# Strided sparse attention and a Mish MLP: the order of batch 1's attention beside the first block's second multiplication

## The chip, the cores and the metric

The kernel runs on one core of a Trainium2 chip. The metric is the device time of one execution in microseconds (us); three runs of the kernel before are given by their median.

A core has a matrix engine (PE, with weight loads shown apart as PEld), a vector engine (DVE), a scalar engine (ACT), a general engine (POOL) and an engine that issues transfers (SP). Each carries out its own instructions in the order of the program, and waits on semaphores for the others.

## The reference

The sizes: 8 batches, 8 heads, 576 positions, head size 64. Heads 0 to 3 are local (a window of 32), heads 4 to 7 strided (every 32nd position).

```python
def _attn_ref(q, k, v):
    scores = scale * np.matmul(q, k.transpose(0, 1, 3, 2))
    rel = pos[:, None] - pos[None, :]
    mask_local = (rel >= 0) & (rel < stride)
    mask_strided = (rel >= 0) & (pos[None, :] % stride == pos[:, None] % stride)
    ...
    attn = np.exp(scores - np.max(scores, axis=-1, keepdims=True))
    attn = attn / (np.sum(attn, axis=-1, keepdims=True) + 1e-09)
    return np.matmul(attn, v)

def _moe_ref(x, w_in, w_out):          # x: 4608 tokens x 512
    h = x @ w_in                       # 512 x 2048
    sp = np.where(h > 20.0, h, np.log1p(np.exp(np.minimum(h, 20.0))))
    g = h * np.tanh(sp)                # Mish
    return g @ w_out                   # 2048 x 512
```

The output of the attention, heads side by side, is the x of the second function.

## The kernel before

The MLP runs over nine blocks of 512 tokens (`t` from 0 to 8). A batch has 576 tokens, so block 1 takes the last 64 tokens of batch 0 and the first 448 of batch 1, which are covered by five local tiles of 96. The attention of batch t + 1 is worked off between the matmul groups of block t. Block 0 multiplies plainly; later blocks use seven products instead of eight for each 2 x 2 split, with sums of weights (`sums_w`, into the tile Tw) and of inputs (`sums_x`, into Sx) prepared on VectorE.

There is no scheduler: the order of the source is the order on every engine. `mlp2` gives 16 groups of four matmuls for block 0 (line 781), and after group i the kernel issues the list `at[i]` that `attn_steps(1, y, y)` returns, with some steps appended:

```python
at[3] += [
    lambda: load_early_v_str(2), lambda: load_tiles_loc(2, kl, k),
    lambda: cast_v_loc(1, Po), lambda: load_tiles_loc(2, ql, q),
]
at[12].append(lambda: transpose_by_dma(2))
at[1].append(lambda: sums_w()[0](lo))
at[7].append(lambda: sums_w()[0](hi))
at[9].append(lambda: sums_w()[1](lo))
at[11].append(lambda: sums_w()[1](hi))
at[14].append(lambda: sums_x(1, "1"))
at[15] += [lambda: spread_v_str(2, Dv)]
```

The steps of batch 1's attention, with their lines:

- `t_step` transposes q or k on PE into a PSUM tile `tr` (strided, line 253: eight transposes; local, line 267: twelve), and one engine copies the tile into kTs, qTs, kTl or qTl (lines 197 and 199). Strided heads come as 72 x 72 pieces, local ones as 96 x 96. k and q of a pair of local heads (`hp` 0 or 1) are one step.
- `Q`, that is `qk`, makes a part of the scores on PE (line 333), in an accumulator of two PSUM banks or, with "t", in two single tiles, and ACT takes the exponential into P_s or P_l (line 347 for an accumulator, line 343, once for each tile, for "t"). The strided scores have three parts (432, 432 and 288 columns for each of two halves), the local ones three as well.
- `M`, that is `mask`, multiplies with the mask on VectorE (line 353).
- `V`, that is `pv`, multiplies with v on PE (line 369, tile `po`), then VectorE takes the reciprocal of the sums (line 380) and the product into x_s or x_l (line 381).
- `spread_v_str` copies v of the strided heads from vsr into vs (line 199); the next load of vsr waits for it.
- `X`, that is `xt`, transposes x_s or x_l on PE (lines 418 and 408, tile `trx`), and a copy puts it into xT, which the MLP reads. `xt_now(n)` does it for n of the six local tiles at once (line 433), and `xt_later(n)` has the rest done by transfers that transpose.

PSUM is scarce: `tile_t` gives one of two single banks in turn, `acc(i, ...)` a tile of two banks, of which there is one for each i. In block 0 both accumulators that `attn_steps` gets are the same one (x == y), and the branch `if x == y` serves this case alone. The kernel library follows reads and writes by tiles and sets the semaphore waits from them.

Of the kernel before, what the change touches and what calls it, by code (L numbers as in the profile page):

```python
# [11 lines left out]
BF16 = mybir.dt.bfloat16  # L12
# [5 lines left out]
WQ = 96  # L18
# [25 lines left out]
def kernel(ctx, tc, q, k, v, moe_w_in, moe_w_out, out):  # L44
    nc = tc.nc
# [13 lines left out]
    xT = const.tile([128, 4, RT], BF16, name="xT")  # L59
# [47 lines left out]
    def acc(i, name):  # L107

        pool = ps_z[0] if i == 2 else ps_a
        return pool.tile([128, 2, 512], F32, tag=f"acc{i}", name=name)  # L110
# [10 lines left out]
    def tile_t(name):  # L121
        return ps_t.tile([128, 512], F32, tag="pt", name=name)
# [11 lines left out]
    def by_head(x):  # L134

        return x[0:PL].rearrange("p j h d -> p (j h d)").rearrange("p (h x) -> p h x", h=4)
# [12 lines left out]
    def vs_raw():  # L149

        return vsr[0:PN]
# [4 lines left out]
    def spread_v_str(b, eng):  # L156
        cast(eng, vs[b % 2][0:PN, :, :, 0:D], vs_raw().rearrange("p h (j d) -> p h j d", d=D))
# [37 lines left out]
    def cast(eng, out_, in_):  # L195
        if eng is nc.scalar:
            nc.scalar.copy(out_, in_)  # L197
        else:
            eng.tensor_copy(out_, in_)
# [42 lines left out]
            eng.memset(vl[b % 2][0:32, 0, :, 0:D], 0.0)  # L242


    def t_step(b, kind, which, hp, eng=None):

        eng = eng or nc.vector
        tr = tile_t("tr")[:].bitcast(BF16)
        if kind == "s":
            src = (qs if which == "q" else ks)[b % 2]  # L250
            for u in range(8):
                h, jj = 2 * hp + u // 4, u % 4
                nc.tensor.transpose(  # L253
                    tr[:, PN * u:PN * u + PN],
                    src[0:PN, h, 128 * jj:128 * jj + 128],
                    ident[0:PN, 0:PN],
                )
            dst = (qTs if which == "q" else kTs)[:, 8 * SU * hp:8 * SU * hp + 8 * SU]
            cast(
                eng, dst.rearrange("c (u n) -> c u n", u=8)[:, :, 0:PN],  # L260
                tr[:, 0:S].rearrange("c (u n) -> c u n", u=8),
            )
        else:
            src = by_head((ql if which == "q" else kl)[b % 2])
            for j in range(CL):
                for e in range(2):
                    nc.tensor.transpose(  # L267
                        tr[64 * e:64 * e + 64, PL * j:PL * j + PL],
                        src[:, 2 * hp + e, D * j:D * j + D], ident[0:PL, 0:PL],
                    )  # L270
            dst = qTl[:, hp, :] if which == "q" else kTl[:, hp, 32:32 + S]
            cast(
                eng, dst.rearrange("c (p j) -> c p j", j=CL),
                tr[:, 0:S].rearrange("c (j p) -> c p j", j=CL),
            )
# [7 lines left out]
    T_ORDER = [(kd, w, hp) for kd in ("s", "l") for hp in range(2) for w in ("k", "q")]  # L283
# [10 lines left out]
    class Attn:  # L294
# [129 lines left out]
                    tr[:, 0:576].rearrange("p (j n) -> p n j", j=CS),  # L424
                )

        def xt_now(self, n):
            tr = tile_t("trx")[:].bitcast(BF16)
            t0 = (self.b % RING) * S
            for c in range(2):  # L430
                for w in range(n):
                    o = (n * c + w) * WQ
                    nc.tensor.transpose(
                        tr[:, o:o + WQ], x_l[0:WQ, w, 128 * c:128 * c + 128], ident[0:WQ, 0:WQ]
                    )
            cast(
                nc.scalar, xT[:, 0:2, t0:t0 + n * WQ],
                tr[:, 0:2 * n * WQ].rearrange("p (c n) -> p c n", c=2),
            )

# [6 lines left out]
    def attn_steps(b, x, y):  # L447

        a = Attn(b)
        Q = lambda i_acc, *parts: (lambda: a.qk(parts, i_acc))  # L450
        M = lambda kd, i: (lambda: a.mask(kd, i, nc.vector))
        V = lambda kd, i: (lambda: a.pv(kd, i))
        X = lambda kd, hf: (lambda: a.xt(kd, hf))
        s0, s1, sl2, l0, l1 = ("s", 0), ("s", 1), (("s", 2), ("l", 2)), ("l", 0), ("l", 1)
        if x == y:
            T = [(lambda n=n, eng=eng: t_step(b, *T_ORDER[n], eng)) for n, eng in enumerate(
                (None, None, None, None, None, nc.scalar, None, nc.scalar))]
            return [
                T[2:4], [Q(x, s0)],
                [M(*s0), Q(x, s1)],  # L460
                [lambda: spread_v_str(b, nc.vector), V("s", 0)],
                [V("s", 1), M(*s1), Q(x, ("s", 2))],
                [V("s", 2), T[4]],
                [V("s", 3), M("s", 2), T[5]],
                [V("s", 4), T[6]],
                [V("s", 5), T[7]],
                [V("s", 6), Q(x, l0)],
                [V("s", 7), M(*l0), Q(x, l1)],
                [X("s", 0), V("l", 0), M(*l1), Q(x, ("l", 2))],
                [X("s", 1), V("l", 1), M("l", 2)],  # L470
                [V("l", 2), V("l", 3)],
                [V("l", 4), V("l", 5)],
                [lambda hf=hf: a.xt("l", hf, nc.vector) for hf in range(2)],
            ], T[0:2]
        V2 = lambda kd, i, z: (lambda: a.pv2(kd, i, z))
        G = lambda kd, i: (lambda: a.mask(kd, i, nc.gpsimd))
        l2 = ("l", 2)
        now = -(-(512 * (b + 1) - S * b) // WQ)
        at = [
            [],  # L480
            [Q(x, s0), Q(y, s1), Q("t", *sl2), M(*s0), M(*s1), M("s", 2)],
            [],
            [V2("s", 0, y), G(*l2)],
            [],
            [V2("s", 2, y), Q(x, l0), Q("t", l1), G(*l0), G(*l1)],
            [],
            [V2("s", 4, y), lambda: nc.scalar.preload_act_table(AF.Mish)],
            [],
            [V2("s", 6, y)],
            [V2("l", 0, x)],  # L490
            [X("s", 0), V2("l", 2, y), X("s", 1)],
            [V2("l", 4, x), lambda: a.xt_now(now)],
            [lambda: a.xt_later(now)],
        ]
        return at
# [364 lines left out]
    with tc.manual_schedule():  # L860
# [43 lines left out]
        a = Attn(0)  # L904
        unread(16)
        cast(Dv, ks[0][0:PN, 0:2, :], st0)
        t_step(0, "s", "k", 0, Sc)
        unread(3, 2)
        t_step(0, "s", "k", 1, Sc)
        ps = [a.bias("s", i, i) for i in range(2)]  # L910
        unread(5, 2)
# [15 lines left out]
        ps = [a.bias("l", 0, 2)]  # L927
# [33 lines left out]
        for t in range(NBLK):  # L961
            if t == 0:
                x, y, z = accs
                at, ts = attn_steps(1, y, y)
                at[3] += [
                    lambda: load_early_v_str(2), lambda: load_tiles_loc(2, kl, k),
# [12 lines left out]
            else:  # L979
                if t == 1:  # L980
                    split_third()
                x, y = 0, 1
                gT, z, g1 = mlp1(t, (y, x) if t == 1 else (x, y))
                at = attn_steps(t + 1, x, y) if t + 1 < B else []
                if t == 1:
                    at[0].append(lambda: sums_w()[3](hi))
# [63 lines left out]
```

## Time and profile before

| what | us |
|---|---|
| median of three runs | 287.01 (286.88 to 287.05) |
| profiled execution | 286.68 |
| its span | 284.8 |
| block 0's second multiplication with batch 1's attention | 35.19 to 57.39 |
| granted clock of TensorE | 1.00 |

The profile is one execution. Its timeline lists instructions with start, duration, engine, line and operands, and in brackets the idle time before and what ended it; the chain of work that ended last is followed back from the last instruction. The shares of the span by engine tell which engine the chain lies on, and a wait counts only there. Starts of matmuls overlap by a little, since they are pipelined; steps are best measured from start to start.

The starts of the 16 groups of block 0 in us: 35.19, 36.58, 37.84, 39.25, 40.31, 41.63, 43.25, 44.72, 46.25, 47.71, 49.12, 50.63, 52.18, 53.45, 54.64, 56.01; block 1 begins at 57.39.

### The profile page before, as it was taken

Reading aid. Unit: us, or ns where it says so; the run is one execution under the profiler, and the core shown is the slowest. Engines: PE = TensorE matmul, PEld = TensorE weight load, DVE = VectorE, ACT = ScalarE, POOL = GpSimd, SP = SyncE. Lnnn points to the kernel's source line nnn. Section 1 sums busy time; section 2 is a strip of 40 time slices with the busy share of each in tenths; the row PEclk is TensorE's granted clock in tenths of the full one; section 3 lists DMA queues with packets and bytes.
Section 4 is the critical chain, followed back from the end, with each engine's and each line's share of the span. In section 5 each row is a group of like instructions: output and inputs, shape, how many; then the busy total and the mean of one; then the engine's idle time right before and its main releaser. Section 6 shows DMA issues by size and latency. Waiting matters only on the chain.

```text
span 284.8 us, 7535 instructions
## 1 busy us (share of the span) xinstructions
PE 279.0 (98%) x3121; PEld 218.6 (77%) x3121; DVE 193.0 (68%) x403; ACT 196.4 (69%) x292; POOL 106.3 (37%) x127
## 2 busy tenths in 40 slices
PE   8999999999999999999999999999999999999995
PEld 3564455586898689868988898788978997888684
DVE  2283067899877777777777778777677767644742
ACT  1578652599867987798779877987699759407820
POOL 8375534406290717271636255345404600000000
PEclk9999999999999999999999999999999999999999
DMA  7999999999989999799999999899979041003004
GB/s 155 185 202 195 190 194 201 143 145 235 169 128 129 214 173 150 139 216 158 155 138 217 122 176 136 216 135 153 157 143 164 4 154 30 0 10 140 0 2 147
DMA packets 103965, 40.73 MB, mean 143 GB/s; under 512 B 86396, under 2 KB 99436, under 8 KB 103932
## 3 DMA queue, kind: packets, MB, share of 16 engines
q1 hardware_dynamic: 67900, 25.13, 51.9%
q0 software_dynamic: 35744, 14.87, 46.8%
q8 instruction: 24, 0.39, 0.6%
q10 hardware_dynamic: 288, 0.25, 0.3%
q14 instruction: 9, 0.07, 0.1%
HBM read 37.20 MB, written 9.44 MB: 164 GB/s over the span
## 4 chain that ended last, share of the span: by engine, by line
PE 92%; DMA 2%; DVE 2%; ACT 1%; issue 0%; ACTq 0%; POOLq 0%
PE pso L748 31%; PE psu L553 10%; PE psh L522 10%; PE psv L553 9%; PE psb L553 8%; PE psb L522 5%; PE po L369 4%; PE pso L808 4%; PE pso L781 4%; PE ps L333 4%; DMA ks<-in_k_dram 2%; PE trx L418 1%; PE un L281 1%; PE tr L267 1%; PE tr L253 1%; DVE x_s L395 1%
## 5 line engine op out<-in xcount | busy, mean ns | idle before, releaser
L748 PEld LDWEIGHTS <-gT 128*128 128x128 bf16 x448 | 41.9, 98 | 5.8
L553 PEld LDWEIGHTS <-w_in 128*128 128x128 bf16 x384 | 37.4, 98 | 8.4
L353 POOL TENSOR_TENSOR Pl<-Pl,consts_sb 128x960 bf16<-128x960 bf16 (+1 forms) x18 | 29.2, 1634 | 38.2 <-issue 22.1
L748 PE MATMUL pso<-w_out,gT 128*128 128x256 bf16 x336 | 40.9, 272 | 0.0
L748 PEld LDWEIGHTS <-Sg 128*128 128x128 bf16 x336 | 31.5, 98 | 4.4
L522 PEld LDWEIGHTS <-w_in 128*128 128x128 bf16 x208 | 20.2, 98 | 16.7 <-issue 0.6
L553 PEld LDWEIGHTS <-Sw 128*128 128x128 bf16 x288 | 28.2, 98 | 3.3
L522 PE MATMUL psh<-xT,w_in 128*128 128x512 bf16 (+1 forms) x136 | 29.4, 366 | 0.2 <-ACT xT L197 0.2
L197 ACT COPY xT<-trx 128x576 bf16<-128x576 bf16 (+3 forms) x24 | 14.2, 629 | 18.4 <-PE trx L418 13.0
L748 PE MATMUL pso<-Tw,Sg 128*128 128x256 bf16 x224 | 26.7, 273 | 0.0
L197 ACT COPY osb<-pso 128x512 f32<-128x512 f32 (+1 forms) x17 | 9.4, 555 | 20.2 <-PE pso L748 10.8
L562 ACT ACTIVATE gT<-psu 128x1024 bf16<-128x1024 f32 x16 | 16.4, 1025 | 8.4 <-PE psu L553 8.4
L395 DVE TENSOR_TENSOR x_s<-po,rden 72x512 bf16<-72x512 f32 x28 | 19.2, 686 | 1.0
L656 DVE TENSOR_TENSOR psu<-psb,p 128x512 f32<-128x512 f32 x16 | 11.2, 700 | 11.8 <-PE psb L553 11.0
L533 ACT ACTIVATE gT<-psh 128x1024 bf16<-128x1024 f32 x16 | 16.2, 1024 | 4.0 <-PE psh L522 3.9
L175 POOL DMA_DIRECT2D vl<-in_v_dram x24 | 17.8, 751 | 2.0 <-issue 1.5
L656 DVE TENSOR_TENSOR Sg<-gT 128x256 bf16<-128x256 bf16 (+2 forms) x32 | 12.8, 422 | 8.0 <-ACT gT L562 6.7
L628 POOL COPY mark<-qTl 1x4 bf16<-1x4 bf16 x6 | 1.6, 268 | 44.4 <-DMA qTl<-ql 44.4
L347 ACT ACTIVATE Ps<-ps 72x864 bf16<-72x864 f32 (+1 forms) x18 | 14.7, 857 | 4.6 <-PE ps L333 4.6
L553 PE MATMUL psu<-xT,w_in 128*128 128x256 bf16 x128 | 17.9, 272 | 0.0
L725 DVE TENSOR_TENSOR p<-pso,p 128x512 f32<-128x512 f32 x14 | 9.6, 685 | 11.9 <-PE pso L748 11.9
L553 PE MATMUL psb<-Sx,w_in 128*128 128x256 bf16 x128 | 17.2, 272 | 0.0
(139 smaller groups left out, 612.8 us busy)
## 6 DMA issues: line engine op xcount, KB each, us to landing
out_dram<-osb SPq DMA_DIRECT2D x9, 512.0 KB, 3.9
out_dram<-p SPq DMA_DIRECT2D x7, 512.0 KB, 3.0
kl<-in_k_dram SPq DMA_DIRECT2D x5, 576.0 KB, 13.6
ql<-in_q_dram SPq DMA_DIRECT2D x5, 576.0 KB, 16.4
qs<-in_q_dram POOLq DMA_DIRECT2D x8, 288.0 KB, 12.0
vsr<-in_v_dram POOLq DMA_DIRECT2D x8, 288.0 KB, 9.0
w_in<-in_moe_w_in_dram POOLq DMA_DIRECT2D x4, 512.0 KB, 9.8
w_out<-in_moe_w_out_dram POOLq DMA_DIRECT2D x4, 512.0 KB, 17.9
```

Of the source, the lines that this page charges most:

```text
L175: nc.gpsimd.dma_start(vl[b % 2][32:128, :, h, 0:D], v[b, h].rearrange("(w p) d -> p w d", p=WQ))
L197: nc.scalar.copy(out_, in_)
L333: nc.tensor.matmul(by_e[e][:, o:o + w], lhsT=lhsT, rhs=rhs, start=not biased, stop=True, skip_group_check=biased,)
L347: nc.scalar.activation(pt[0:n, :, 0:nw], ps[0:n, :, o0:o0 + nw], AF.Exp, scale=scale)
L353: meng.tensor_tensor(out=pm, in0=pm, in1=mk[0:n, :].unsqueeze(1).unsqueeze(1).to_broadcast([n, 2, nu, w]), op=ALU.mult,)
L395: nc.vector.tensor_tensor(out=dst.rearrange("p e (h d) -> p e h d", h=4), in0=po[0:m, :, :, 0:D], in1=rden[0:m].unsqueeze(3).to_broadcast( ...
L522: nc.tensor.matmul(ps_u[:, o:o + n], lhsT=w_in[:, cc, fc * 128:(fc + 1) * 128], rhs=xT[:, cc, a:a + n], start=(cc == 2 and (o == 0 or len( ...
L533: nc.scalar.activation(to, tiles[g][:], AF.Mish)
L553: nc.tensor.matmul(p[:, 256 * j:256 * j + 256], lhsT=lhs[:, cc, f:f + 128], rhs=rhs[:, cc], start=(first and j == 0 and cc == 0), stop=(la ...
L562: nc.scalar.activation(gT[:, c:c + src.shape[1], 256 * half_t:256 * half_t + 256], src, AF.Mish,)
L656: nc.vector.tensor_tensor(out=out_, in0=in0, in1=in1, op=op)
L748: nc.tensor.matmul(ps[:, pair, :], lhsT=lhs(c, 128 * pair), rhs=rhs(c), start=(first and pair == 0 and c == 0), stop=(last and c == 7), sk ...
```

## The change

For batch 1 alone: the two first strided score parts are issued one behind the other after group 1, the second in two single tiles, with both masks behind them, and the spread of v stands alone after group 2; the transposes of local k of both head pairs are issued in one step after group 5, those of local q after group 7, each pair in one accumulator tile of two banks, whose first bank VectorE copies out and whose second ScalarE does; and at the end five tiles of the local x are transposed and copied at once, the sixth by a transfer.

```diff
-    def t_step(b, kind, which, hp, eng=None):
+    def t_step(b, kind, which, hp, eng=None, ps=None):
...
-        tr = tile_t("tr")[:].bitcast(BF16)
+        tr = (tile_t("tr")[:] if ps is None else ps).bitcast(BF16)
...
-        def xt_now(self, n):
+        def xt_now(self, n, eng=nc.scalar):
...
             cast(
-                nc.scalar, xT[:, 0:2, t0:t0 + n * WQ],
+                eng, xT[:, 0:2, t0:t0 + n * WQ],
...
         if x == y:
-            T = [(lambda n=n, eng=eng: t_step(b, *T_ORDER[n], eng)) for n, eng in enumerate(
-                (None, None, None, None, None, nc.scalar, None, nc.scalar))]
+            T = [(lambda n=n: t_step(b, *T_ORDER[n])) for n in range(4)]
+
+            def t_pair(which):
+                tr = acc(x, "tr")
+                for hp, eng in enumerate((nc.vector, nc.scalar)):
+                    t_step(b, "l", which, hp, eng, tr[:, hp, :])
+
             return [
-                T[2:4], [Q(x, s0)],
-                [M(*s0), Q(x, s1)],
-                [lambda: spread_v_str(b, nc.vector), V("s", 0)],
-                [V("s", 1), M(*s1), Q(x, ("s", 2))],
-                [V("s", 2), T[4]],
-                [V("s", 3), M("s", 2), T[5]],
-                [V("s", 4), T[6]],
-                [V("s", 5), T[7]],
+                T[2:4],
+                [Q(x, s0), Q("t", s1), M(*s0), M(*s1)],
+                [lambda: spread_v_str(b, nc.vector)],
+                [V("s", 0)],
+                [V("s", 1), Q(x, ("s", 2))],
+                [V("s", 2), M("s", 2), lambda: t_pair("k")],
+                [V("s", 3)],
+                [V("s", 4), lambda: t_pair("q")],
+                [V("s", 5)],
                 [V("s", 6), Q(x, l0)],
                 [V("s", 7), M(*l0), Q(x, l1)],
                 [X("s", 0), V("l", 0), M(*l1), Q(x, ("l", 2))],
                 [X("s", 1), V("l", 1), M("l", 2)],
                 [V("l", 2), V("l", 3)],
                 [V("l", 4), V("l", 5)],
-                [lambda hf=hf: a.xt("l", hf, nc.vector) for hf in range(2)],
+                [lambda: a.xt_now(5, nc.vector), lambda: a.xt_later(5)],
             ], T[0:2]
```

## The prediction

> **What bounds the kernel now.** I read the busy shares first, then the chain that ended last as shares, then the chain and the timeline from 33 to 61 us, the stretch of block 0's second multiplication, which holds the whole change. "Step n" is group n of `mlp2` with the list `at[n]` behind it.
>
> ```profile
> PE 279.0 (98%) x3121; PEld 218.6 (77%) x3121; DVE 193.0 (68%) x403; ACT 196.4 (69%) x292; POOL 106.3 (37%) x127
> ...
> PE 92%; DMA 2%; DVE 2%; ACT 1%; issue 0%; ACTq 0%; POOLq 0%
> ```
>
> TensorE (PE) is busy 98% and carries 92% of the chain. Its instructions run in program order, so any time in which its next one waits is added to the end unless a later wait gives it back. Inside the stretch the chain leaves PE once in its first half:
>
> ```profile
> 37.61 0.32 PE ps L333 x12
> ...
> 38.01 0.90 ACT Ps L347
> 38.91 0.04 issue
> 38.95 0.37 PE ps L333 x12
> ```
>
> The second score part waits until the exponential of the first has freed the one accumulator that both use. Group 2 would have ended at 38.70 (start 37.84, four matmuls of 0.216), so this wait costs 0.25. The timeline has the orders that the sum needs:
>
> ```profile
> 37.26 0.68 DVE L656 TENSOR_TENSOR Tw<-w_out 128x1024 bf16<-128x1024 bf16 x1
> ...
> 38.01 0.89 ACT L347 ACTIVATE Ps<-ps 72x864 bf16<-72x864 f32 x1 [0.81 <-PE ps L333]
> ...
> 38.93 0.60 DVE L353 TENSOR_TENSOR Ps<-Ps,consts_sb 72x864 bf16<-72x864 bf16 x1 [0.99 <-ACT Ps L347]
> ...
> 39.46 0.68 DVE L199 COPY vs<-vsr 72x2048 bf16<-72x2048 bf16 x1
> ...
> 40.19 0.28 PE L369 MATMUL po<-vs,Ps 72*128 72x65 bf16 x4
> ...
> 41.80 0.65 ACT L347 ACTIVATE Ps<-ps 72x576 bf16<-72x576 f32 x1 [1.50 <-PE ps L333]
> ...
> 42.87 0.45 PE L267 MATMUL tr<-consts_sb,Sg 96*64 96x96 bf16 x12
> ...
> 42.98 0.18 DVE L380 RECIPROCAL rden<-po 72x4 f32<-72x4 f32 x1 [0.33 <-PE po L369]
> 43.19 0.42 DVE L381 TENSOR_TENSOR x_s<-po,rden 72x256 bf16<-72x256 f32 x1
> ...
> 43.53 0.74 DVE L199 COPY kTl<-tr 128x576 bf16<-128x576 bf16 x1
> ...
> 44.34 0.45 PE L267 MATMUL tr<-consts_sb,Sg 96*64 96x96 bf16 x12
> ```
>
> To see here: VectorE (DVE) does the weight sum Tw while it would only wait for the exponential, then the mask, then the spread of v; the first PV (V s0) starts 0.05 after the spread ends (39.46 + 0.68 = 40.14). And no transpose waits for a copy: each run of 12 has a PSUM tile of its own, and its copy comes out beside the next matmuls.
>
> **Steps 1 to 3: the score parts together.** In the changed order both score parts stand in step 1, the second in two tiles, so its 0.25 wait is gone. But `at[1]` gets its weight sum appended at the end, and the two masks now stand ahead of it. DVE's order becomes mask s0, mask s1, Tw, spread; before it was Tw, mask s0, spread, with mask s1 two PVs later. Behind mask s1, which waits, are queued the Tw sum and the spread, and PE waits for the spread. The exponential of s0 still ends at 38.90. Then come two of 72x432, a shape that the trace has not:
>
> ```profile
> L343 ACT ACTIVATE Ps<-ps 72x288 bf16<-72x288 f32 x12 | 4.2, 407 | 0.0
> ```
>
> The size lies midway between this and the 72x576 at 41.80 above, so 0.53 each (bounds 0.41 and 0.65). At 73.94 us two of 72x288 take 0.70 together, so a second starts 0.11 before the first ends: 38.90 + 2 x (0.53 - 0.10) = 39.75. Mask s1 starts at 39.79; from a mask's start to the next DVE start is 0.53 (38.93 to 39.46), from a Tw's 0.61 (53.21 to 53.82). Tw starts at 40.32, the spread at 40.93, and ends at 41.61. V s0 at 41.66 instead of 40.19: **+1.47** (+1.2 to +1.8 by the bounds). PE itself is ready far sooner: step 1 ends at about 38.04, groups 2 and 3 at 39.77, so the longer step 1 (12 more small matmuls, 0.2) costs nothing and PE stands for 1.9 us. The cover that hid Tw, the wait for the first exponential, is what is lost.
>
> **Steps 5 and 6: local k as a pair.** The text of the change says one run of 24 transposes. Both halves are now one tile of two banks, and in the built program the 13th transpose waits for VectorE's copy of the first half, the copy on ScalarE (ACT) for that too. So it is two runs of 12 with a DVE copy between them, on PE's path. That copy is queued on DVE behind V s2's reciprocal and product and mask s2, which the change puts ahead of it. From V s2's start: reciprocal +0.33, product +0.21, mask +0.34 (product 0.42 less 0.08 by which DVE instructions overlap, as 43.19 to 43.53), copy +0.36 (a 72x576 mask, 0.44 less 0.08): it starts at +1.24, takes 0.74 and lets PE go 0.05 later, at +2.03. Twelve transposes take 0.38 (44.34 to group 7 at 44.72), so group 6 starts at V s2 + 2.41. Before, from V s2 to group 6 it was 0.74 (42.51 to 43.25, with 0.14 of waiting for mask s1, which goes). So +1.67. Step 6 loses its run and shrinks from 1.47 to 0.99 (group 0.87, PV 0.12): -0.48. Together **+1.19**. ScalarE's half copy (0.64) lies beside the next group.
>
> **Steps 7 and 8: local q likewise.** Ahead of the copy are only V s4's two instructions: 0.32 + 0.21 + 0.34 = 0.87, a copy of 0.74, 0.05, 0.38: group 8 at V s4 + 2.04, before 0.66 (45.59 to 46.25). +1.38, and step 8 goes from 1.46 to 0.99: -0.47. Together **+0.91**. DVE never copied qTl in this trace; the same shape into kTl took 0.748 and the unscattered 128x576 qTs copy 0.451. I take the first, which has the same stride; the other would take off 0.3.
>
> **Rest of the stage.** Steps 4 and 9 to 14 keep their order, and the order of DVE in them, so they move as a block. The loads on POOL move with the spread (vsr is issued after it, then kl, ql, whose slots wait for earlier landings anyway). GpSimd's cast of v follows them, at most 1.5 later than its end at 50.0, while V l0 moves from 51.76 to about 55.3: hidden.
>
> **Last step: five tiles.** Ten transposes instead of twelve at 0.043 (0.52 for 12): **-0.09**. One DVE cast of 128x960 replaces two of 128x576 (0.82 for both, 0.45 one; so between 0.45 and 0.82, I take 0.66), starts 0.17 later since it needs all ten, and ends at the same point. The next sum on the path (Sx, ended at 59.08) is first used at 60.05, so 0.9 us hide it; without that cover it would cost those 0.2. The sixth tile becomes one DMA transpose on SP behind the two output stores at 64.1 and ahead of the loads for batch 3: 1.2 to 2.0 of the queue. Block 1 ends before these tokens, so only block 2, near 87, reads it: nothing.
>
> Sum: 1.47 + 1.19 + 0.91 - 0.09 = +3.48. The profiled execution took 286.68 (span 284.8, 1.9 around it), so it would become 290.2; the median of the runs shown, 287.01, is 0.33 above it, so 290.5. By the bounds, with up to 0.1 for PE's restart after each of three stands (12 score matmuls took 0.30 after a wait, where 32 in a row took 0.53): 289.9 to 291.2.
>
> **Rivals.** *The clock falls in the stands.* PE would stand for 1.9, 1.5 and 1.1 us within 10 us. At the start of the trace, after idleness, matmuls came every 0.43 until 5.0 us and then every 0.21:
>
> ```profile
> 1.60 0.15 PEld L281 LDWEIGHTS <-Tw 128*128 128x128 bf16 x1 [0.27 <-issue]
> 2.03 0.15 PEld L281 LDWEIGHTS <-Tw 128*128 128x128 bf16 x1 [0.28 <-issue]
> ```
>
> Nine at twice the price are 1.9 us, so one such spell would give 292.4. Against it: no stand as long as these is in the trace between matmuls, so neither side is shown, but half of those 10 us is still matmuls. The Trainium skill, "TensorE: Matmul & The Clock Gate", section "Why this matters for your kernels", warns of idle gaps above about 3 us; by that rule none of the three is long enough and the sum stays, while the granted clock of 1.00 throughout this trace cannot test it.
>
> *The halves do not wait for each other* (the copies free PE bank by bank, the change doing what it says). Then 24 transposes take 0.69 in one go, and group 6 comes 0.91 after V s2, group 8 as long after V s4: +0.17 - 0.48 + 0.25 - 0.47, and with 1.47 and -0.09 the total is +0.85, or 287.9. The wait in the program speaks against it.
>
> *The delay is given back* (not slower). If batch 2's operands were what block 1's scores wait for, PE could stand 3.5 us here for nothing, and the time stays at 287.0. It decides where the last landing of qTl comes later than the 72.50 at which PE reads it:
>
> ```profile
> 65.98 0.72 POOL L628 COPY mark<-qTl 1x4 bf16<-1x4 bf16 x1 [10.47 <-DMA qTl<-ql]
> ...
> 72.50 0.25 PE L333 MATMUL ps<-qTl,kTl 64*128 64x96 bf16 x4
> ```
>
> It lands 6.5 us before, so this would need transfers far later than now.
>
> *Only the merging counts* (faster): waits hidden and four switches into transposes made two, 0.25 + 0.1 of steps 1 and 2, 0.46 of steps 5 to 8 and 0.09: 286.1. DVE's order speaks against it.
>
> **How the numbers follow.** Forecast 0.79, falling clock 0.09, halves free 0.05, given back 0.04, merging 0.03. The time is the forecast's, 290.5. The range runs from its lower end, widened by 0.5 because three terms lean on one order, to the clock's case: 289.4 to 292.6; left out are 0.12 and a remnant of the forecast. This kernel's measurement tells 0.2%, 0.57 us, from no change: slower is 0.79 + 0.09 + 0.05 = 0.93, same 0.04, faster 0.03.
>
> **What would show it.** In the changed profile: a Tw sum between mask s1 and the spread, and V s0 near 41.7 with PE idle 1.9 before it; PE idle about 1.5 in the middle of the k transposes and 1.1 in the q transposes, both ended by a DVE copy of kTl or qTl; block 1's first matmul near 60.9 instead of 57.39; all later stages at their old length. The forecast is wrong if the transposes show no gap, if the spread ends before 40.5, or if a later stage is shorter by microseconds.

## The result, and the profile after

The changed kernel takes 290.57 us (median of four runs, 290.44 to 290.67) against 286.94 for the kernel before (286.75 to 287.05): ratio 1.0126, 95% interval 1.0113 to 1.0138. It is slower by 3.6 us. The profiled execution took 290.63, with a span of 288.8 against 284.8 and a granted clock of 1.00.

On the page the busy times hardly change, since the same work is done, but PE's share of the span falls:

```profile
PE 279.0 (97%) x3119; PEld 218.3 (76%) x3119; DVE 191.6 (66%) x402; ACT 196.3 (68%) x293; POOL 104.7 (36%) x127
...
PE 79%; DMA 10%; DVE 4%; POOL 2%; ACT 2%; issue 2%; SPq 1%; POOLq 0%; ACTq 0%
```

PE is busy for 279.0 as before, in a span 4.0 longer: it stood. The second line, the chain's shares, misleads here. Followed back from 150.5 us it leaves PE at one small wait (0.17, shown below) and runs mostly along transfers and GpSimd for 27 us in which PE was busy too. The timeline of the stage is the better guide:

```profile
38.83 0.93 ACT L343 ACTIVATE Ps<-ps 72x432 bf16<-72x432 f32 x2
...
39.79 0.60 DVE L353 TENSOR_TENSOR Ps<-Ps,consts_sb 72x864 bf16<-72x864 bf16 x1 [0.23 <-ACT Ps L343]
40.32 0.68 DVE L662 TENSOR_TENSOR Tw<-w_out 128x1024 bf16<-128x1024 bf16 x1
40.92 0.69 DVE L199 COPY vs<-vsr 72x2048 bf16<-72x2048 bf16 x1
...
41.66 0.30 PE L369 MATMUL po<-vs,Ps 72*128 72x65 bf16 x4 [1.70 <-DVE vs L199]
...
45.23 0.75 DVE L199 COPY kTl<-tr 128x576 bf16<-128x576 bf16 x1
46.03 0.45 PE L267 MATMUL tr<-consts_sb,Sg 96*64 96x96 bf16 x12 [1.38 <-DVE kTl L199]
...
49.15 0.74 DVE L199 COPY qTl<-tr 128x576 bf16<-128x576 bf16 x1
...
49.95 0.45 PE L267 MATMUL tr<-consts_sb,Sg 96*64 96x96 bf16 x12 [1.01 <-DVE qTl L199]
...
60.92 1.04 PE L559 MATMUL psu<-xT,w_in 128*128 128x256 bf16 x8
61.12 0.66 DVE L199 COPY xT<-trx 128x960 bf16<-128x960 bf16 x1 [0.17 <-PE trx L433]
```

The brackets on PE's lines are the three stands of the stage: PE waits 1.70 until VectorE has spread v, 1.38 until VectorE has copied the first half of k's transposes, 1.01 until that of q's. Block 1 starts at 60.92 instead of 57.39. Against group 1's start (36.61, before 36.58) that is 3.50 later. It is less than the three stands together, since the change also saves small waits and switches.

Two small losses come afterwards. In block 4 ScalarE starts a copy 0.28 later after its previous instruction than before, and PE waits for it; the block takes 29.22 instead of 28.94. First the timeline of the changed kernel, then of the kernel before:

```profile
149.43 1.06 ACT L584 COPY psb<-psu 128x512 f32<-128x512 f32 x2 [0.62 <-PE psu L559]
...
150.54 0.60 PE L559 MATMUL psu<-xT,w_in 128*128 128x256 bf16 x4 [0.17 <-ACT psb L584]
```

```profile
145.61 1.06 ACT L578 COPY psb<-psu 128x512 f32<-128x512 f32 x2 [0.34 <-PE psu L553]
```

And at block 6's start a sum on VectorE takes 1.04 while GpSimd casts q, and PE goes on at 207.23, about 0.2 late. Before, that sum took 0.41 (second fence):

```profile
206.08 1.78 POOL L199 CAST ql<-ql 96x768 bf16<-96x768 f32 x2 [1.82 <-DMA ql<-in_q_dram]
206.13 1.04 DVE L662 TENSOR_TENSOR Sx<-xT 128x512 bf16<-128x512 bf16 x1
...
207.23 0.77 PEld L559 LDWEIGHTS <-Sw 128*128 128x128 bf16 x8 [0.34 <-DVE Sx L662]
```

```profile
202.31 0.41 DVE L656 TENSOR_TENSOR Sx<-xT 128x512 bf16<-128x512 bf16 x1
```

### The profile page after: what moved, and what is told of

Its sections match the earlier page's. It is cut to its first block, busy times and chain, and to the rows that moved or that the text cites. A ratio compares the mean times of both kernels' runs of the same rounds, so it can differ in the third digit from the quotient of the medians.

```text
span 288.8 us, 7534 instructions
## 1 busy us (share of the span) xinstructions
PE 279.0 (97%) x3119; PEld 218.3 (76%) x3119; DVE 191.6 (66%) x402; ACT 196.3 (68%) x293; POOL 104.7 (36%) x127
## 3 DMA queue, kind: packets, MB, share of 16 engines
q0 software_dynamic: 35744, 14.87, 45.8%
## 4 chain that ended last, share of the span: by engine, by line
PE 79%; DMA 10%; DVE 4%; POOL 2%; ACT 2%; issue 2%; SPq 1%; POOLq 0%; ACTq 0%
PE pso L754 25%; PE psh L528 9%; PE psu L559 9%; PE psv L559 7%; PE psb L559 7%; DMA kl<-in_k_dram 5%; PE pso L814 4%; PE psb L528 4%; PE po L369 4%; DMA ql<-in_q_dram 4%; PE pso L787 3%; PE ps L333 3%; DMA kTl<-kl 1%; PE trx L418 1%; POOL Pl L353 1%
## 5 line engine op out<-in xcount | busy, mean ns | idle before, releaser
L568 ACT ACTIVATE gT<-psu 128x1024 bf16<-128x1024 f32 x16 | 16.4, 1024 | 8.5 <-PE psu L559 8.5
L347 ACT ACTIVATE Ps<-ps 72x864 bf16<-72x864 f32 (+1 forms) x17 | 13.8, 854 | 6.1 <-PE ps L333 6.1
```

Of the source, the lines that this page charges most:

```text
L347: nc.scalar.activation(pt[0:n, :, 0:nw], ps[0:n, :, o0:o0 + nw], AF.Exp, scale=scale)
L568: nc.scalar.activation(gT[:, c:c + src.shape[1], 256 * half_t:256 * half_t + 256], src, AF.Mish,)
```

## The experiments

The theory: VectorE's order makes the first PV late, and the shared tile makes PE wait for a copy twice. Each experiment mends one of them, or makes one part of the change alone. A gain is the changed kernel's median, 290.57, less that of the kernel in question; a ratio is to the kernel before, which was run beside it each time (medians 286.84 to 286.94); starts are read against group 1's, because the whole stage begins up to 0.7 later or earlier from one profile to another.

**One weight sum earlier** (the changed kernel, with one line moved):

```diff
-                at[1].append(lambda: sums_w()[0](lo))
+                at[0].append(lambda: sums_w()[0](lo))
```

> The changed kernel with the first weight sum (Tw) issued one step earlier, so that VectorE does it before both masks, as in the kernel before; the spread of v stays behind mask s1. Theory (VectorE's order): mask s1 still starts near 39.8, the spread follows it at 40.3 instead of 40.9 and ends at 41.0, so the first PV starts at 41.05 instead of 41.66: 0.6 less than the changed kernel, about 290.0. Rival (the second score part's exponential, now two instructions on ScalarE, holds the PV back, and VectorE's order does not matter): first PV stays at 41.7, time stays at 290.6.

Measured 290.15, ratio to the kernel before 1.0115 (1.0098 to 1.0132). In the trace the first PV starts at 41.38, with group 1 0.32 later than in the changed kernel: 0.60 gained, and block 1 starts 0.61 sooner by the same measure. The timed gain is 0.42. In the profiled execution the stage began 0.32 later, which takes back part of the 0.61; what it is in the others was not seen. VectorE's order counts; the exponentials alone don't hold the PV.

**The spread of v ahead of both masks** (with the line above):

```diff
-                [Q(x, s0), Q("t", s1), M(*s0), M(*s1)],
-                [lambda: spread_v_str(b, nc.vector)],
+                [Q(x, s0), Q("t", s1), lambda: spread_v_str(b, nc.vector), M(*s0), M(*s1)],
+                [],
```

> The changed kernel with Tw and the spread of v both ahead of the two masks on VectorE; the pairs of transposes stay as changed. Theory (VectorE's order): the spread ends near 38.6, the first PV needs only mask s0, done at 39.53, and starts when group 3 ends, near 39.8: 1.86 less than the changed kernel, 288.7, with the two gaps in the transposes (1.5 and 1.1 us) unchanged. Rival (the two exponentials): first PV not before 39.8 to 40.4 because ScalarE ends them at 39.75, so up to 0.6 of the 1.86 stays. Rival (something after the stage eats or adds time): the time moves by something else than the first PV does.

Measured 288.62 (1.0061, 1.0046 to 1.0076): 1.95 gained. The timeline, PE's lines:

```profile
38.83 1.24 PE L787 MATMUL pso<-w_out,gT 128*128 128x512 bf16 x5
39.90 0.29 PE L369 MATMUL po<-vs,Ps 72*128 72x65 bf16 x4
```

No bracket: the PV follows group 3 at once (1.86 sooner, group 1 being 0.10 later). The two gaps in the transposes are unchanged, 1.38 and 1.01.

**Two tiles for each pair** (the changed kernel):

```diff
-                for hp, eng in enumerate((nc.vector, nc.scalar)):
-                    t_step(b, "l", which, hp, eng, tr[:, hp, :])
+                t_step(b, "l", which, 0, nc.vector, tr[:, 0, :])
+                t_step(b, "l", which, 1, nc.scalar)
```

> The changed kernel, but the second half of each pair of transposes goes to a single PSUM tile of its own instead of the second bank of the same tile. Theory (the wait is set by the tile, not by the hardware): the 24 transposes run in one go, group 6 comes 0.9 after the PV of step 5 instead of 2.4, group 8 0.9 instead of 2.0 after that of step 7: 2.6 less, 288.0; the first PV stays at 41.7. Rival (PE cannot write transposes while VectorE reads the other bank, or the transposes are slow after a PV): the gap of about 1.4 us stays or becomes slower transposes, and the time stays within 0.5 of 290.6.

Measured 287.89 (1.0035, 1.0022 to 1.0048): 2.7 gained. PE's timeline now shows one run of 24, and group 6 comes 0.85 after the PV:

```profile
44.07 0.29 PE L369 MATMUL po<-vs,Ps 72*128 72x65 bf16 x4
44.29 0.70 PE L267 MATMUL tr<-consts_sb,Sg 96*64 96x96 bf16 x24
44.92 1.04 PE L787 MATMUL pso<-w_out,gT 128*128 128x512 bf16 x4
```

So the wait came from the tile: once the halves are separate tiles, PE writes the second without waiting for the copy of the first. VectorE begins that copy only at 45.31, when the transposes are over, so this run does not show whether PE could write one bank while VectorE reads the other.

**The engines of the copies swapped** (the changed kernel, `enumerate((nc.scalar, nc.vector))`):

> The changed kernel with the engines of the pairs swapped: ScalarE copies the first half, VectorE the second; still one tile. Theory (PE waits for the copy of the first half, and that copy for what is queued ahead of it on VectorE): ScalarE is idle, its copy starts 0.54 after the first transposes and takes 0.64, so PE goes on 1.45 after the PV instead of 2.04 for k and 1.68 for q: 0.8 less, 289.8. Rival (the wait is for the tile as such, whoever copies, or for VectorE's mask): unchanged, 290.6.

Measured 289.48 (1.0113, 1.0070 to 1.0155): 1.1 gained by the median. The ratio and its wide interval contain one execution of the four that took 292.14, with a granted clock of 0.986; the others took 289.45 to 289.49, at 0.998 to 1.00. PE goes on 1.39 after the PV for k, 1.44 for q:

```profile
44.20 0.28 PE L369 MATMUL po<-vs,Ps 72*128 72x65 bf16 x4
...
45.59 0.45 PE L267 MATMUL tr<-consts_sb,Sg 96*64 96x96 bf16 x12 [0.73 <-ACT kTl L197]
```

The gap is what the first copy and the queue ahead of it take, here on ScalarE, whose queue is empty. The 0.3 beyond the forecast is the size of the loss in block 4, which is absent here (a gap of 0.34).

**One part alone.** The kernel before with the score parts in their new order only:

> Of the change only the two score parts together; transposes and the last step as in the kernel before. Theory (VectorE's order): first PV at 41.7 as in the changed kernel (+1.47), the wait of the third PV for mask s1 gone (-0.14), nothing given back: +1.3 at the start of block 1, so it starts at 58.7. A second, smaller loss is seen in the four kernels with the change's score parts: in block 4 ScalarE starts the copy psb<-psu 0.62 after its last instruction instead of 0.34, and PE loses 0.28. If that comes from the one more instruction that ScalarE has (the second exponential in two), it is here too, and the time is about 288.5; if it comes from the one more transfer on SP, it is not, and the time is about 288.3. Rival (the stand at the first PV is made up in the later steps): the time stays at 287.0 to 287.5.

with the paired transposes only:

> Of the change only the paired transposes (with mask s2 ahead of them); score parts and the last step as in the kernel before. Theory (waits set by the tile, the copy queued on VectorE): group 6 at 1.8 later than before, step 6 shorter by 0.48, group 8 1.38 later, step 8 shorter by 0.47: +2.24 in all, 289.2. ScalarE has as many instructions as before and SP as many transfers, so the loss of 0.28 in block 4 is absent by either reading. Rival (the pairs only lose because the late first PV leaves VectorE behind): about +0.5, 287.5.

and with the last step only:

> Of the change only the last step: five local tiles of x in one group and the sixth by a transfer. Theory: two transposes less, -0.09, below what the time can tell: 286.85, same. For the 0.28 in block 4: here SP has one more transfer and ScalarE no more instructions, so the gap before ScalarE's copy psb<-psu in block 4 is 0.62 if the transfer sets it and 0.34 if the instruction does. Rival (one cast of 960 that waits for all ten transposes is late): block 1's second product waits, +0.2.

Measured 288.39 (1.0049, 1.0034 to 1.0064), 289.21 (1.0075, 1.0059 to 1.0092) and 286.88 (0.9997, 0.9988 to 1.0007): +1.46, +2.28 and -0.05 on 286.93. They add up to 3.69, where the whole change cost 3.63, each known to some 0.3 to 0.5: within that the parts do not help or hinder each other, and nothing is made up later. In their traces block 1 starts 1.26, 2.27 and -0.13 later against group 1. The gap in block 4 is 0.62 in the first and 0.34 in the other two, so the additional transfer doesn't set it.

**Both mends together** (spread first and two tiles):

> Both mends together: Tw and the spread ahead of the masks, and two tiles for each pair. Theory: the two add up, 4.5 less than the changed kernel, 286.1; but group 8 would then be due at 46.0, while the third quarter of w_out landed about 46.2 in the kernel before, so up to 0.3 may stay as a wait for that transfer: 286.1 to 286.4, thus 0.5 to 0.8 below the kernel before. Rival (the merging of runs saves nothing in itself): equal to the kernel before, 286.9 to 287.0.

Measured 286.55 (0.9988, 0.9973 to 1.0003), not to be told from the kernel before, and scattered from 285.51 to 287.41. Its profiled execution took 285.89, with no wait left on PE in the stage but 0.1 or so: from group 1 to block 1 it takes 19.65, before 20.81. So without its two waits the new order does save time in the stage, 1.15 here. The granted clock was 0.999 or 1.00 in all ten executions, so it does not make the scatter. What may make some of them longer, the next two runs show.

**The same with one idle instruction more on ScalarE** (`at[6].append(lambda: Sc.copy(mark[:], ident[0:1, 0:4]))`):

> Both mends together (as e4_both) and one idle instruction more on ScalarE, a copy of four constants in step 6. Two questions. First, block 4: in the kernels where ScalarE's copy psb<-psu of block 4 is number 192 of its instructions, counted from 0, the gap before it was 0.62, where it is 191 or 193 it was 0.34. Theory (the place in the instruction stream sets it): number 193 here, gap 0.34, 0.28 less than with e4_both. Rival (the later PE or the transfers set it): 0.62. Second, the spread of e4_both's times (285.5 to 287.4, where the kernel before has 286.4 to 287.2): theory: group 8 waits for the third quarter of w_out, which landed between 45.6 and 47.5 over the profiles so far, so this profile either has it landing before 45.8 and a stage that ends near 56.4, or a wait of PE before group 8 as long as the landing is late. Rival: the scatter comes from a later block. Median 286.0 to 286.4.

Measured 285.92 (0.9973, 0.9964 to 0.9982): faster than both kernels, 0.27% below the kernel before. The gap in block 4 is 0.34. And group 8 waits for weights (the landing times in the expectation are starts of GpSimd's next transfer that waits for this landing, which come about 0.5 after PE is let go):

```profile
46.07 1.02 PE L787 MATMUL pso<-w_out,gT 128*128 128x512 bf16 x3 [0.16 <-DMA w_out<-in_moe_w_out_dram]
```

**The same as both mends, with the stage's last weight sum later** (`sums_w()[1](hi)` from `at[11]` to the head of the last steps of `at[15]`):

> Both mends together (as e4_both), and the last weight sum of the stage (Tw, 0.68 on VectorE in step 11) moved behind the last step. Theory: in steps 12 to 14 PE waits a little for VectorE's products (x_l), which this sum delays; without it up to 0.3 less in the stage, while the sum Sx in block 1 comes 0.6 later and still before PE reads it (0.9 of room): 286.2 to 286.4 by the median of e4_both, again with the spread of the landing of w_out. Rival: the room in block 1 is not there and the 0.3 is paid back.

Measured 286.49 (0.9986, 0.9977 to 0.9994). From group 12 to block 1 it takes 5.12, as in the run above, so moving the sum gained nothing in its stage, and one product of block 1 takes 1.08 instead of 0.95: the forecast was wrong. Without the sum the weight loads of those steps still wait for VectorE's products (0.22 and 0.27 for x_l). What this profile gives is group 8, in an execution of 286.96:

```profile
46.66 0.38 PE L787 MATMUL pso<-w_out,gT 128*128 128x512 bf16 x1 [0.69 <-DMA w_out<-in_moe_w_out_dram]
```

With both mends group 8 is due at 45.8, and the third quarter of w_out was there in time (execution of 285.89), at 46.0 (285.92) or at 46.6 (286.96). In the kernel before, group 8 was due when it landed, at 46.2. So the stage has a second bound close behind the first, and the landing scatters; that fits with the median, in which 4.0 us show of the 4.5 that the two mends are worth alone (by their ratios, 0.0065 and 0.0091 of 286.94). It is not shown to be all of it: over the thirteen profiles that quarter landed between 45.0 and 47.0, at most 1.2 after 45.8, and the slowest execution of both mends took 1.5 more than the profiled one. How often the weights were late in the executions without a profile was not seen.

**Both mends, the load of v started later** (the small transfer ahead of it reads `w_in[0:1, 0, 1536:1792]` instead of `1024:1280`):

> Both mends together (as e4_both), with the load of v for the local heads of batch 1 started one quarter of w_in later, since the small transfer ahead of it waits for the last quarter instead of the third. Theory (the third quarter of w_out sets group 8): with the queue of that load out of the way for longer, w_out lands sooner, group 8 does not wait and the times scatter less, 285.6 to 286.2, unless v itself then comes too late for the first local PV near 50.9 (GpSimd's cast has to end before it), which would show as a wait there of up to 1. Rival (the loads do not bound the stage): same as e4_both, with its scatter.

Measured 289.53 (1.0086, 1.0050 to 1.0123), scattered from 287.28 to 291.46. Group 8 doesn't wait in its profile (an execution of 287.71), but v is late, and the scatter is larger, not smaller:

```profile
52.63 0.29 PE L369 MATMUL po<-vl,Pl 128*128 128x65 bf16 x4 [1.60 <-POOL vl L242]
```

Both loads are needed at nearly the same time here, and in this profile what one gains the other more than loses. The scatter is another matter: it goes with the granted clock. Three executions took 287.28 to 287.71 at 0.998 or 1.00, three 289.45 to 290.09 at 0.994, two 291.38 and 291.46 at 0.987 and 0.986. An estimate from these figures: 0.006 and 0.0135 of a span of 288 are 1.7 and 3.9 us, near the 2.2 and 3.9 by which the second and third group lie above the first. What lowered the clock is not shown; no such execution has a profile.

## Why the prediction was right

It gave 290.5 in a range of 289.4 to 292.6, slower with 0.93. Point by point:

- *VectorE's order*, +1.47: the first PV was put at 41.66 and started at 41.66. Mask s1 at 39.79, Tw at 40.32 and the spread at 40.92 came within 0.01 of where the sum had them; the two exponentials of the unseen shape took 0.93 together, the estimate 0.96.
- *Local k as a pair*, from the PV to group 6 2.41: 2.42 (43.99 to 46.41). Step 6 0.99: 1.00.
- *Local q*, 2.04: 2.06 (48.27 to 50.33). Step 8 0.99: 0.99. The copy of qTl on VectorE took 0.74, the upper of the two rows that bounded it.
- *The last step*, -0.09: its transposes take 0.43 (60.49 to 60.92) instead of 0.52. The cast took 0.66 and nobody waited for it.
- *The stands*, put at 1.9, 1.5 and 1.1: 1.87, 1.45 and 1.08 if counted from start to start as the sum does. The brackets (1.70, 1.38, 1.01) count from the ends of the pipelined matmuls and are smaller.
- *The sum*: +3.48 to the start of block 1, measured +3.50.
- *"All later stages at their old length"* is the step that failed, by little: 0.28 in block 4 and about 0.2 in block 6 of this profile. The first is in all eight kernels in which ScalarE's copy has the same place among its instructions (below); the second is a meeting of two engines in this execution, since in the other twelve profiles that sum takes 0.41 to 0.43.
- *The time*, 290.5 for 290.57: that it is so near is in part luck. The two profiled executions differ by 3.95, the medians by 3.63 (3.2 to 4.0 by the interval), and the loss in block 4 was not in the sum.

The rivals: *the clock falls* did not happen in the changed kernel. Three stands of 1.70, 1.38 and 1.01 us left it at 0.999 or 1.00 in all four executions, and the group after the first stand takes 0.86 in the chain, as any other. The Trainium skill, "TensorE: Matmul & The Clock Gate", section "Why this matters for your kernels", warns of gaps above about 3 us; the trace agrees with that, though no profile here has a gap that long. The rival was no empty one: with the engines swapped one execution of four, and with the later v five of eight, had a granted clock of 0.994 or less. How long PE stood in these was not seen. *The halves do not wait* was priced at +0.85; with two tiles the stage is 0.73 longer than before, so the price was about right and only its condition was not met. *The delay is given back* and *only the merging counts* fall with the parts run alone; the saving that the latter priced at 0.9 is real, as both mends show, but two waits outweigh it here.

## What to carry to other kernels

Where every engine works in program order, a step that is pulled forward takes along what stands behind it: ask of each instruction that now waits what is queued after it, and who waits for that (here a weight sum and a spread behind a mask). Merging runs gains only if the halves have tiles of their own, for the wait is set by the tile. And when a stall is taken away, look what lands or is copied just behind it: here the weights landed up to 0.7 us after they were then needed, which took back part of the gain.

## What the runs showed of the hardware

- ScalarE's gap before the copy `psb<-psu` of block 4 was 0.34 or 0.62, and its place in ScalarE's instructions tells the cases apart: 0.62 in the eight kernels in which it is number 192 in the trace, counted from 1 with those that only wait or issue, where the expectation counts from 0 (among them the score parts alone and both mends), 0.34 in those in which it is number 191 (the kernel before, the pairs alone, the last step alone) or 193 (the swap, the additional instruction). What lies behind that place was not shown.
- VectorE's sum of two 128x512 operands took 0.41 alone and 1.04 when a cast of GpSimd had begun 0.05 before. The Trainium skill, "SBUF — State Buffer", section "Who interferes with whom", says that a VectorE instruction with two inputs in SBUF and a GpSimd instruction that reads SBUF exclude each other, the later one waiting for the earlier; the trace goes that way, though not quite the whole of it: the sum is 0.63 longer, and waiting out one of the two casts (1.78 together) would have cost 0.84.
